# Block-causal attention with a top-2 expert layer: rebuilt with wide q/k rows, exponentials as stationary operand, one scatter of rows, and a dense expert stage in two halves

## Chip, cores and metric

One core of one Trainium2 chip runs the whole program: one launch, inputs in DRAM, output in DRAM. The metric is the device time of one execution in microseconds (us); for the kernel before it is the median of three runs.

## What is computed

The reference in short (B=8, H=8, S=576, D=64; N=4608 tokens, Dm=512, E=8 experts, F=1024):

```python
scores = q @ k.T / sqrt(64)                 # per batch and head
mask   = block_i >= block_j                 # blocks of 64 positions
attn   = softmax(where(mask, scores, -1e9)) @ v
x      = attn as (N, 512)
noisy  = x @ w_gate + log1p(exp(x @ w_noise)) * noise
top2, top2_w = two largest of noisy, softmax over the two
out[n] = sum over both: top2_w * relu(x[n] @ w1[e]) @ w2[e]
```

The inputs are drawn once with a fixed seed. In this draw, with the tokens split by batch into two halves of 2304 (batches 0 to 3, 4 to 7), the largest number of tokens that one expert gets in one half is 624, the smallest 540.

## The kernel before

Everything is scheduled by a tile framework: engines run their own queues, and a tile pool's buffer count sets how far one step may run ahead of the next. The order on each engine's queue is the framework's, made from the code's order and its own estimate of when things are ready.

**Attention** (lines 109 to 205) goes batch by batch. POOL loads q, k and v in 128-row pieces, as 64-element rows per head (L124 to L128, cast to bf16 on the way). PE transposes q and k, two heads at a time (L143, L146), ACT copies the transposes out of PSUM (L149, L151), DVE lays v out with a column of ones (L153, L154). For each head and key tile `jt`, PE makes scores of up to 512 columns with the keys as the stationary operand (L169, contraction over 64 rows, in the lower or the upper row half by the head's parity), ACT takes the exponential (L175) and DVE zeroes the one masked block (L181). L190 then multiplies exponentials (stationary) with v and its ones; DVE divides by the summed column (L197, L198). The rows go to DRAM as `x_bf`.

**Routing** (211 to 347) reads x back tile by tile (L237), transposes it (L240), computes logits (L245), and on six groups of tiles the softplus, the two maxima and the weights. ACT loads function tables as it goes (L252, L253, L272). Positions within each expert come from two matmuls and a scan over all 4608 tokens (L282 to L304). 72 indirect DMAs on POOL write a small record of every token into eight record tables (L329); these are loaded, added and stored as one (L341 to L347).

**Experts** (349 to 435): 8 experts with a capacity of 1280 rows each, in steps of 512, 512 and 256 rows (24 steps, 10240 rows). A step reads its records (L382), gathers its x rows by 128 on POOL (L385), transposes them on PE (L409; ACT copies, L411), computes relu(x w1) with w1 stationary (L417, L420) and the product with w2 (L425), and writes rows to `y_den` (L430, L432). Up to four steps are gathered ahead, and weights come in three buffers (L368, L371).

**Combine** (437 to 453): for each of 36 token tiles POOL gathers two rows per token from `y_den` (L442), DVE scales and adds (L450 to L452), SP writes the output (L453). The gathers stand behind all of `y_den`'s writes.

Of the kernel before, what the change touches and what calls it, by code (L numbers as in the profile page):

```python
# [8 lines left out]
F32 = mybir.dt.float32  # L10
BF16 = mybir.dt.bfloat16
I32 = mybir.dt.int32
U32 = mybir.dt.uint32
AF = mybir.ActivationFunctionType
ALU = mybir.AluOpType


@with_exitstack
def kernel(
# [19 lines left out]

    P = 128  # L40
    NST = (S + P - 1) // P
    s_sizes = [min(P, S - i * P) for i in range(NST)]
    CAP = 1280
    NCT = CAP // P
    BREC = E * CAP + P
    DB = Dm // P
    FB = F // P
    NT = N // P
    NK = 2
    NC = NK * NT  # L50

    x_bf = nc.dram_tensor("x_bf16", (N, Dm), BF16, kind="Internal").ap()
    w1_bf = nc.dram_tensor("w1_bf", (E, Dm, F), BF16, kind="Internal").ap()
    w2_bf = nc.dram_tensor("w2_bf", (E, F, Dm), BF16, kind="Internal").ap()
    bucket_rec = nc.dram_tensor("bucket_rec", (BREC, 4), F32, kind="Internal").ap()
    M = 8
    CHLEN = (NK * (N // P)) // M
    assert (BREC * 4) % P == 0
    BRW = BREC * 4 // P
    rec_m = [nc.dram_tensor(f"rec_m{m}", (BREC, 4), F32, kind="Internal").ap()  # L60
             for m in range(M)]

    consts = ctx.enter_context(tc.tile_pool(name="consts", bufs=1))

    ident_f32 = consts.tile([P, P], F32)
    make_identity(nc, ident_f32)
    ident_bf = consts.tile([P, P], BF16)
    nc.vector.tensor_copy(ident_bf, ident_f32)

    ustrict = consts.tile([P, P], BF16)  # L70
    nc.gpsimd.memset(ustrict, 0.0)
    nc.gpsimd.affine_select(
        out=ustrict, in_=ustrict, compare_op=ALU.is_ge, fill=1.0,
        base=0, pattern=[[-1, P]], channel_multiplier=1,
    )
    ones_mat = consts.tile([P, P], BF16)
    nc.vector.memset(ones_mat, 1.0)

    ecap_i = consts.tile([P, 1, E], I32)
    nc.gpsimd.iota(ecap_i, pattern=[[0, 1], [CAP, E]], base=0, channel_multiplier=0)  # L80
    ecap = consts.tile([P, 1, E], F32)
    nc.vector.tensor_copy(ecap, ecap_i)

    negbig = consts.tile([P, 1], F32)
    nc.vector.memset(negbig, -1.0e9)

    wgn = consts.tile([P, DB, 2 * E], BF16)
    nc.gpsimd.dma_start(out=wgn[:, :, 0:E],
                        in_=moe_w_gate.rearrange("(b p) e -> p b e", p=P))
    nc.gpsimd.dma_start(out=wgn[:, :, E:2 * E],  # L90
                        in_=moe_w_noise.rearrange("(b p) e -> p b e", p=P))

    y_den = nc.dram_tensor("y_den", (E * CAP, Dm), BF16, kind="Internal").ap()

    keep = ctx.enter_context(tc.tile_pool(name="keep", bufs=1))
    boffi_k = keep.tile([P, NC], I32)
    wA_k = keep.tile([P, NK, NT], F32)

    with tc.tile_pool(name="zero", bufs=1) as zpool:
        brz = zpool.tile([P, BRW], F32)  # L100
        nc.vector.memset(brz, 0.0)
        for m in range(M):
            nc.scalar.dma_start(
                out=rec_m[m].rearrange("a b -> (a b)").rearrange("(p w) -> p w", p=P),
                in_=brz)

    x_attn_view = x_bf.rearrange("(b s) (h d) -> b h s d", b=B, h=H)

    with tc.tile_pool(name="qkv", bufs=2) as qkv_pool, \
         tc.tile_pool(name="head", bufs=2) as head_pool, \  # L110
         tc.tile_pool(name="awork", bufs=2) as work_pool, \
         tc.tile_pool(name="xacc", bufs=2) as xacc_pool, \
         tc.tile_pool(name="a_tr_ps", bufs=2, space=bass.MemoryType.PSUM) as tr_psum, \
         tc.tile_pool(name="a_sc_ps", bufs=2, space=bass.MemoryType.PSUM) as sc_psum, \
         tc.tile_pool(name="a_av_ps", bufs=4, space=bass.MemoryType.PSUM) as av_psum:

        for b in range(B):
            q_sb = qkv_pool.tile([P, NST, H, D], BF16, tag="q_sb")
            k_sb = qkv_pool.tile([P, NST, H, D], BF16, tag="k_sb")
            v_sb = qkv_pool.tile([P, NST, H, D], BF16, tag="v_sb")  # L120
            for st in range(NST):
                sl = s_sizes[st]
                ss = st * P
                nc.gpsimd.dma_start(out=q_sb[:sl, st],  # L124
                                  in_=q[b, :, ss:ss + sl, :].rearrange("h s d -> s h d"))
                nc.gpsimd.dma_start(out=k_sb[:sl, st],
                                  in_=k[b, :, ss:ss + sl, :].rearrange("h s d -> s h d"))
                nc.gpsimd.dma_start(out=v_sb[:sl, st],  # L128
                                    in_=v[b, :, ss:ss + sl, :].rearrange("h s d -> s h d"))

            xacc = xacc_pool.tile([P, NST, Dm], BF16, tag="xacc")

            HG = H // 2
            SP = NST * P
            qTa = head_pool.tile([P, HG, SP], BF16, tag="qTa")
            kTa = head_pool.tile([P, HG, SP], BF16, tag="kTa")
            vext5 = head_pool.tile([P, NST, H, D + 1], BF16, tag="vext5")
# [346 lines left out]
```

## Time and profile before

| | us |
|---|---|
| median of three runs (lowest, highest) | 978.03 (977.12, 979.61) |
| span of the profiled execution, first to last instruction | 976.8 |
| PE busy / ACT busy / POOL busy / DVE busy | 629.8 / 412.1 / 343.2 / 243.4 |

The profile is one execution; its page gives no time of its own beside the span, which lies 1.2 us below the median. A busy share is the time in which an engine had an instruction in work. The forty-slice lines show it by stage (a slice is 24.4 us), the chain of waits follows the last instruction back to what it waited for, and the groups by line give the mean duration of one instruction; an idle time has behind it what ended it. PE matmuls overlap in the pipeline, so that a mean duration is longer than the distance from one start to the next.

### The profile page before, as it was taken

What the parts mean: (1) busy time and instruction counts of PE and PEld (TensorE: products, weight loads), DVE (VectorE), ACT (ScalarE), POOL (GpSimd) and SP (SyncE); (2) the same over time, 40 slices, a digit from 0 to 9 for tenths busy, and PEclk for the clock granted to TensorE, in tenths of its full rate; (3) what the DMA queues carried; (4) which work ended last, traced back from release to release, by engine and by line L of the source; (5) the groups of instructions that cost most, each with busy time, mean ns of one, the idle gap of its engine ahead of it and who ended that gap; (6) DMA issues with size and microseconds to landing.
All of it is one profiled execution on the core that took longest, in us unless ns stands there. A gap on an engine that the chain in (4) does not pass through costs nothing.

```text
span 976.8 us, 11092 instructions
## 1 busy us (share of the span) xinstructions
PE 629.8 (64%) x3684; PEld 316.5 (32%) x3684; DVE 243.4 (25%) x1207; ACT 412.1 (42%) x904; POOL 343.2 (35%) x373
## 2 busy tenths in 40 slices
PE   2999999999997550000006899889889888940000
PEld 1544544444443330000002444444444444420000
DVE  1555555555553125000100000000000000015665
ACT  2665565665554781000003555555555555520000
POOL 7945414500000002777434123231312300027775
PEclk9999999999999999999997999999999999985555
DMA  9999849910002320000497372644627210015665
GB/s 132 141 99 79 71 49 88 76 31 25 1 25 55 96 76 1 2 2 2 69 211 138 82 147 73 141 99 108 138 72 146 70 44 33 22 65 178 192 199 172
DMA packets 181578, 84.27 MB, mean 86 GB/s; under 512 B 138128, under 2 KB 167952, under 8 KB 181520
## 3 DMA queue, kind: packets, MB, share of 16 engines
q0 software_dynamic: 135712, 51.04, 40.7%
q1 hardware_dynamic: 33616, 25.13, 8.7%
q10 hardware_dynamic: 12192, 7.38, 2.6%
q8 instruction: 29, 0.48, 0.2%
q14 instruction: 29, 0.24, 0.1%
HBM read 88.18 MB, written 26.28 MB: 117 GB/s over the span
## 4 chain that ended last, share of the span: by engine, by line
PE 56%; issue 13%; ACT 10%; DMA 8%; POOL 8%; DVE 2%; another core or an unknown queue 1%; ACTq 0%; SPq 0%; POOLq 0%; DVEq 0%
PE yp L425 14%; PE hp L417 12%; PE ps L169 12%; PE av L190 11%; POOL rec_m L329 4%; ACT xgT L411 4%; POOL yg L442 3%; DMA yg<-y_den,boffi_k 2%; DMA xt<-x_bf 2%; PE tp L409 2%; DMA xg<-x_bf,gidx 2%; PE tpq L143 2%; ACT esc L175 2%; PE tpk L146 2%; ACT hsb L420 1%
## 5 line engine op out<-in xcount | busy, mean ns | idle before, releaser
L175 ACT ACTIVATE esc<-ps 128x512 bf16<-128x512 f32 (+5 forms) x384 | 140.3, 392 | 112.9 <-PE ps L169 86.4
L417 PE MATMUL hp<-xgT,w1sb 128*128 128x512 bf16 (+1 forms) x768 | 165.2, 350 | 21.0 <-ACT hsb L420 9.6
L385 POOL DMA_INDIRECT xg<-x_bf,gidx x80 | 76.8, 960 | 200.6 <-PE tp L409 102.3
L169 PE MATMUL ps<-qTa,kTa 64*128 64x512 bf16 (+5 forms) x384 | 141.6, 403 | 7.5 <-ACT esc L175 6.3
L190 PE MATMUL av<-vext,esc 128*128 128x65 bf16 (+2 forms) x960 | 143.7, 246 | 0.5 <-DVE xacc L198 0.4
L425 PE MATMUL yp<-w2sb,hsb 128*128 128x512 bf16 x640 | 143.5, 379 | 0.0
L409 PE MATMUL tp<-ident_bf,xg 128*128 128x128 bf16 x320 | 34.7, 222 | 159.5 <-DMA xg<-x_bf,gidx 140.1
L411 ACT ACTIVATE xgT<-tp 128x512 bf16<-128x512 bf16 (+1 forms) x96 | 50.6, 527 | 170.7 <-PE tp L409 161.2
L329 POOL DMA_INDIRECT rec_m<-recA,boffi_k x72 | 70.3, 976 | 144.7 <-DVE boffi_k L323 123.1
L420 ACT ACTIVATE hsb<-hp 128x512 bf16<-128x512 f32 (+1 forms) x192 | 98.6, 526 | 47.8 <-PE hp L417 36.0
L190 PEld LDWEIGHTS <-esc 128*128 128x128 bf16 (+2 forms) x960 | 83.1, 123 | 101.1 <-DVE xacc L198 26.8
L442 POOL DMA_INDIRECT yg<-y_den,boffi_k x72 | 77.0, 1070 | 105.8 <-issue 102.8
L417 PEld LDWEIGHTS <-w1sb 128*128 128x128 bf16 x768 | 72.6, 99 | 81.2 <-issue 36.8
L409 PEld LDWEIGHTS <-xg 128*128 128x128 bf16 x320 | 26.2, 98 | 185.8 <-DMA xg<-x_bf,gidx 140.7
L450 DVE TENSOR_SCALAR acc<-yg,wA_k 128x512 f32<-128x512 bf16 x36 | 18.7, 518 | 271.7 <-DMA yg<-y_den,boffi_k 270.5
L425 PEld LDWEIGHTS <-hsb 128*128 128x128 bf16 x640 | 62.5, 98 | 73.5 <-issue 0.9
L430 ACT ACTIVATE ysb<-yp 128x512 bf16<-128x512 f32 x80 | 47.8, 598 | 88.9 <-PE yp L425 88.9
L198 DVE TENSOR_SCALAR xacc<-av,denom 128x64 bf16<-128x64 f32 (+1 forms) x320 | 82.3, 276 | 5.0
L197 DVE RECIPROCAL denom<-av 128x1 f32<-128x1 f32 (+1 forms) x320 | 52.4, 165 | 105.7 <-PE av L190 102.4
L128 POOL DMA_DIRECT2D v_sb<-in_v_dram x40 | 36.0, 901 | 60.7 <-DVE xacc L198 60.7
L169 PEld LDWEIGHTS <-kTa 64*128 64x128 bf16 (+1 forms) x384 | 35.5, 108 | 34.2 <-issue 14.1
L124 POOL DMA_DIRECT2D q_sb<-in_q_dram x40 | 35.9, 897 | 24.2 <-PE ps L169 12.8
(81 smaller groups left out, 392.2 us busy)
## 6 DMA issues: line engine op xcount, KB each, us to landing
out_dram<-acc SPq DMA_DIRECT2D x36, 256.0 KB
w1sb<-in_moe_w_dram POOLq DMA_DIRECT2D x8, 1024.0 KB
w2sb<-in_moe_w_dram POOLq DMA_DIRECT2D x8, 1024.0 KB
y_den<-ysb SPq DMA_DIRECT2D x40, 128.0 KB
y_den<-ysb ACTq DMA_DIRECT2D x40, 128.0 KB
xt<-x_bf SPq DMA_DIRECT2D x36, 128.0 KB
q_sb<-in_q_dram POOLq DMA_DIRECT2D x32, 128.0 KB
k_sb<-in_k_dram POOLq DMA_DIRECT2D x32, 128.0 KB
```

The lines of the kernel that those rows point to most:

```text
L169: nc.tensor.matmul(out=ps[:jl, :cn], lhsT=kTa[po:po + D, g, jt * P:jt * P + jl], rhs=qTa[po:po + D, g, i0 + off:i0 + off + cn], start=True ...
L175: nc.scalar.activation(out=esc[:jl, jt, off:off + cn], in_=ps[:jl, :cn], func=AF.Exp, scale=1.0 / (D ** 0.5),)
L190: nc.tensor.matmul(out=av[:il, :], lhsT=esc[:jl, jt, loc:loc + il], rhs=vext5[:jl, jt, h, :], start=(jt == 0), stop=(jt == ib),)
L198: nc.vector.tensor_scalar_mul(xacc[:il, ib, h * D:(h + 1) * D], av[:il, 0:D], denom[:il])
L329: nc.gpsimd.indirect_dma_start(out=rec_m[m], out_offset=bass.IndirectOffsetOnAxis(ap=boffi[:, c:c + 1], axis=0), in_=recA_f[:, c, :], in_o ...
L385: nc.gpsimd.indirect_dma_start(out=xg[:, ci, :], out_offset=None, in_=x_bf, in_offset=bass.IndirectOffsetOnAxis(ap=gidx[:, ci:ci + 1], axi ...
L409: nc.tensor.transpose(tp[:, ci * P:(ci + 1) * P], xg[:, ci, db * P:(db + 1) * P], ident_bf)
L411: nc.scalar.activation(out=xgT[:, db, 0:QW], in_=tp[:, 0:QW], func=AF.Copy)
L417: nc.tensor.matmul(out=hp[:, 0:QW], lhsT=w1sb[:, db, fb * P:(fb + 1) * P], rhs=xgT[:, db, 0:QW], start=(db == 0), stop=(db == DB - 1))
L420: nc.scalar.activation(out=hsb[:, fb, 0:QW], in_=hp[:, 0:QW], func=AF.Relu)
L425: nc.tensor.matmul(out=yp, lhsT=hsb[:, fb, ci * P:(ci + 1) * P], rhs=w2sb[:, fb, :], start=(fb == 0), stop=(fb == FB - 1))
L442: nc.gpsimd.indirect_dma_start(out=yg[:, kk, :], out_offset=None, in_=y_den, in_offset=bass.IndirectOffsetOnAxis(ap=boffi_k[:, c:c + 1], a ...
```

## The change

The program is written anew. Two batches make a group `g` (four groups), two groups make a half.

- q and k are loaded as contiguous rows of 512 elements, which hold eight successive positions of one head. PE transposes 64x128 pieces so that batch 2g lands in row half 0 and batch 2g+1 in row half 64; DVE copies 1024 columns at a time and undoes the interleaving of positions by a strided write (new line 172). v is loaded straight into its tile with the ones.
- Scores of the two batches alternate between the two row halves of PE (new line 233) into one PSUM tile of 2 x 512 columns, on which ACT takes one exponential of 1024 elements a partition (237). Key tiles of 320 and 192 columns share a tile. AV accumulates four heads in one PSUM tile (261, and 275 for the last 64 positions), DVE divides four heads at once.
- The rows of a group stay in SBUF (`xr`). Router transposes (288), logits (292), and positions (one matmul pair and one scan a group, with a running base per half) follow at once. `exp` and `ln` come from one preloaded table; the second weight is the reciprocal of 1 plus an exponential.
- Each token's row is scattered by two indirect DMAs a tile (357; 72 in all) directly into expert buckets of 640 rows, one DRAM array `xd` a half. SP writes zeros over both arrays at the start (2 x 5.2 MB), so that unused rows hold zeros. Rows beyond 640 would go to an overflow area.
- Experts run dense: for each half and expert one plain load of 640 rows (380), 20 transposes (392), four DVE copies of 640 columns (393), 64 matmuls of 320 columns (399), 40 of 512 (407), DVE copies (410), SP writes. All weights stay in SBUF: experts 0 and 1 in their own space, loaded during attention, 2 to 7 in space that attention held.
- The combine of half 0 is issued after its eighth expert, that of half 1 at the end (36 gathers each, line 419; two DVE operations a tile, 424 and 425).
- At the end the largest count is loaded into a register, and a branch computes overflow rows if it is above 640.

The core of the diff (the whole of the old body goes):

```diff
+    for lo, hi in ((0, 1), (4, 6), (1, 4), (6, 9)):
+        nc.gpsimd.dma_start(out=qr[:, lo:hi, :], in_=qv[:, t0 + lo:t0 + hi, :])
+        nc.gpsimd.dma_start(out=kr[:, lo:hi, :], in_=kv[:, t0 + lo:t0 + hi, :])
...
+    nc.tensor.transpose(tp[64 * hf:64 * hf + 64, r * n:(r + 1) * n],
+                        raw[p0:p0 + n, src_t, r * 64:(r + 1) * 64],
+                        ident[p0:p0 + n, p0:p0 + n])
...
+    for u in range(3):
+        sc = sc_ps.tile([P, 2, 512], F32, tag="sc")
+        for jt, a, z, off in pieces[u]:
+            for hf in range(2):
+                c0 = col0(hf, h)
+                sl = slice(64 * hf, 64 * hf + 64)
+                nc.tensor.matmul(out=sc[:, hf, off:off + z - a],
+                                 lhsT=kT[sl, c0 + jt * P:c0 + jt * P + P],
+                                 rhs=qT[sl, c0 + a:c0 + z], start=True, stop=True)
+        nc.scalar.activation(out=esc[:, hh, :, u * 512:(u + 1) * 512], in_=sc,
+                             func=AF.Exp, scale=scale)
...
+    ins = nc.gpsimd.indirect_dma_start(
+        out=xd[half], out_offset=bass.IndirectOffsetOnAxis(
+            ap=slots[:, t0 + idx, i:i + 1], axis=0),
+        in_=xr[:, idx, :], in_offset=None, bounds_check=XR - 1, oob_is_err=False)
...
+    seq = [(half, e) for half in range(NH) for e in range(E)]
+    xgs = {0: load_x(*seq[0]), 1: load_x(*seq[1])}
+    for e in range(2, E):
+        load_w(wL, e)
+    for i, (half, e) in enumerate(seq):
+        if i + 2 < len(seq):
+            xgs[i + 2] = load_x(*seq[i + 2])
+        expert(half, e, xgs.pop(i))
+        if i == E - 1:
+            combine(0)
+    combine(1)
+    over = nc.values_load(flag_i[0:1, 0:1], min_val=0, max_val=1)
+    with tc.If(over > 0):
...
```

Two places of the order. On POOL's queue, from the end of attention on, before (`rec_m` are the record tables, `xg` an expert step's x rows, `yg` the combine's rows):

```order
L221 IOTA recA 128x72
L329 DMA rec_m<-recA,boffi_k 10368x4 x72
L368 DMA w1sb<-in_moe_w_dram 128x4x1024
L371 DMA w2sb<-in_moe_w_dram 128x8x512
L368 DMA w1sb<-in_moe_w_dram 128x4x1024
L371 DMA w2sb<-in_moe_w_dram 128x8x512
L385 DMA xg<-x_bf,gidx 128x512 x20
```

and now, from the scatters of groups 1 and 2 on:

```order
L357 DMA xd<-xr,slots 9728x512 x36
L115 DMA w_2_3721<-in_moe_w_dram 128x4x1024
L117 DMA w_2_3723<-in_moe_w_dram 128x8x512
L115 DMA w_3_3725<-in_moe_w_dram 128x4x1024
L117 DMA w_3_3727<-in_moe_w_dram 128x8x512
L357 DMA xd<-xr,slots 9728x512 x18
L115 DMA w_4_3729<-in_moe_w_dram 128x4x1024
...
L117 DMA w_7_3743<-in_moe_w_dram 128x8x512
L419 DMA yg<-yd,gslots 128x512 x72
```

The 72 indirect writes of a stage of their own became 72 scatters that stand group by group between the loads, the 80 gathers of x rows are gone, and all 72 combine gathers follow the last weight load. On DVE's queue, at the first combine, before (behind the last expert step's index conversion):

```order
L383 CAST gidx<-brt 128x4 x2
L383 CAST gidx<-brt 128x2
L450 TENSOR_SCALAR acc<-yg,wA_k 128x512
L451 TENSOR_SCALAR tmp<-yg,wA_k 128x512
L452 TENSOR_TENSOR acc<-acc,tmp 128x512
```

and now, between the x copies of the first expert of half 1 and those of the second:

```order
L393 COPY xgT<-tp 128x640 x4
L424 TENSOR_SCALAR acc<-yg,wts 128x512
L425 SCALAR_TENSOR_TENSOR acc<-yg,wts,acc 128x512
...
L424 TENSOR_SCALAR acc<-yg,wts 128x512
L410 CAST ysb<-yp 128x512
...
L410 CAST ysb<-yp 128x512
L425 SCALAR_TENSOR_TENSOR acc<-yg,wts,acc 128x512
L393 COPY xgT<-tp 128x640 x4
L410 CAST ysb<-yp 128x512 x5
```

All 36 operations of the first combine (18 tiles) stand there in one run, with the five `ysb` casts of one expert among them, the first behind the eighth tile, and the x copies of the next expert (`xgT`) behind all of them.

## Rows read from the trace of the kernel before

**Rows 1.** Page, the span in 40 slices: PE and its granted clock, in tenths.

```profile
PE   2999999999997550000006899889889888940000
PEclk9999999999999999999997999999999999985555
```

**Rows 2.** Windows by stage: length, then busy us (instructions) of PE, PEld, DVE, ACT, POOL; PEclk, DMA share, GB/s.

```profile
25.00:150.00 125.00, 122.25 (x738) 61.42 (x736) 65.86 (x415) 76.83 (x206) 63.92 (x78) 1.00 1.21 89
310.00:382.00 72.00, 30.79 (x292) 19.41 (x292) 22.21 (x86) 44.99 (x71) 0.00 (x0) 1.00 0.27 73
382.00:480.00 98.00, 0.00 (x0) 0.00 (x0) 1.02 (x3) 0.00 (x0) 70.26 (x72) 1.00 0.10 15
600.00:700.00 100.00, 89.78 (x514) 45.80 (x512) 0.34 (x2) 55.71 (x111) 28.62 (x31) 1.00 0.49 109
868.00:977.00 109.00, 0.40 (x2) 0.00 (x0) 59.00 (x108) 0.60 (x1) 77.02 (x72) 0.51 0.55 176
...
500.00:540.00 40.00, 20.07 (x78) 8.35 (x79) 2.56 (x14) 8.80 (x16) 15.51 (x17) 0.83 0.94 171
```

**Rows 3.** Chain of waits in order of time: start us, us, what.

```profile
9.02 0.89 POOL q_sb L124
...
491.64 19.01 DMA xg<-x_bf,gidx
...
551.37 6.92 PE yp L425 x32
561.46 1.03 PE hp L417 x8
...
604.33 1.03 PE hp L417 x8
...
869.07 1.70 DMA y_den<-ysb
...
969.05 3.18 DMA yg<-y_den,boffi_k
```

**Rows 4.** Groups by line and shape: busy us, mean ns of one, idle before and releasers.

```profile
L190 PE MATMUL av<-vext,esc 128*128 128x65 bf16 x640 | 101.1, 241 | 0.0
L169 PE MATMUL ps<-qTa,kTa 64*128 64x512 bf16 x64 | 38.7, 604 | 0.0
L175 ACT ACTIVATE esc<-ps 128x512 bf16<-128x512 f32 x64 | 38.3, 598 | 50.6 <-PE ps L169 31.1 <-issue 5.5 <-ACT esc L175 5.2
L175 ACT ACTIVATE esc<-ps 128x64 bf16<-128x64 f32 x64 | 14.2, 222 | 14.7 <-PE ps L169 13.2
L409 PE MATMUL tp<-ident_bf,xg 128*128 128x128 bf16 x320 | 34.7, 222 | 159.5 <-DMA xg<-x_bf,gidx 140.1 <-ACT xgT L411 19.4
L143 PE MATMUL tpq<-ident_bf,q_sb 128*128 128x128 bf16 x128 | 23.1, 304 | 16.3 <-DMA q_sb<-in_q_dram 16.3
L198 DVE TENSOR_SCALAR xacc<-av,denom 128x64 bf16<-128x64 f32 x256 | 65.6, 277 | 3.5
L294 DVE COPY scanA<-tot_ps 128x576 f32<-128x576 f32 x1 | 0.8, 750 | 0.0
L256 DVE TENSOR_TENSOR noisy<-noisy,lg 128x48 f32<-128x48 f32 x6 | 1.2, 204 | 0.6
```

**Rows 5.** Timeline of PE within attention: start us, us, engine, line, what.

```profile
109.96 0.34 PE L190 MATMUL av<-vext,esc 128*128 128x65 bf16 x3
110.24 0.26 PE L169 MATMUL ps<-qTa,kTa 64*64 64x64 bf16 x1
...
112.29 0.23 PE L169 MATMUL ps<-qTa,kTa 64*128 64x64 bf16 x1
112.29 0.23 PE L143 MATMUL tpq<-ident_bf,q_sb 64*128 64x64 bf16 x1
```

**Rows 6.** Timeline of POOL, first and last of the 72 combine gathers.

```profile
871.79 1.02 POOL L442 DMA_INDIRECT yg<-y_den,boffi_k  x1 [84.21 <-issue]
...
969.05 1.39 POOL L442 DMA_INDIRECT yg<-y_den,boffi_k  x1 [0.31 <-issue]
```

More of the change, by code (lines that the diff above doesn't have):

```diff
@@ L87 @@
[L87 to L97, printed above, removed]
@@ new lines, with token_rows @@
+    NG = B // 2
+    TG = 9
+    NT = NG * TG
+    NH = 2
+    TH = NT // NH
+    CAP = 640
+    CT = CAP // P
+    NW = CAP // 2
+    OVB = E * CAP
+    XR = OVB + 2 * TH * P
+    BIG = float(1 << 20)
+    SET = 4
+    EO = (0, 576, 1024, 1344)
+    ESC = 1536
+    scale = 1.0 / (D ** 0.5)
+    xd = [nc.dram_tensor(f"xd{i}", (XR, Dm), BF16, kind="Internal").ap() for i in range(NH)]
+    yd = [nc.dram_tensor(f"yd{i}", (OVB, Dm), BF16, kind="Internal").ap() for i in range(NH)]
+    def token_rows(g, idx):
+        if idx < 8:
+            b = 2 * g + idx // 4
+            return [(0, P, b * S + (idx % 4) * P)]
+        return [(64 * hf, 64, (2 * g + hf) * S + 512) for hf in range(2)]
@@ new lines, with setup_consts @@
+    ecap_i = consts.tile([P, E, 1], I32)
+    rmask = consts.tile([P, E, TG], F32)
+    ovrow_i = consts.tile([P, 2, TH], I32)
+    ovrow = consts.tile([P, 2, TH], F32)
+    base = [consts.tile([P, E, 1], F32, name=f"base{i}") for i in range(NH)]
+    nz_all = keep.tile([P, NT, E], F32)
+    slots = keep.tile([P, NT, 2], I32)
+    gslots = keep.tile([P, NT, 2], I32)
+    wts = keep.tile([P, 2, NT], F32)
+    oh_all = keep.tile([P, NG, 2, E, TG], BF16)
+    zero = keep.tile([P, 2048], BF16)
+    def setup_consts():
+        make_identity(nc, ident_f)
+        nc.vector.tensor_copy(ident, ident_f)
+        nc.gpsimd.memset(prem, 0.0)
+        nc.gpsimd.affine_select(out=prem, in_=prem, compare_op=ALU.is_gt, fill=-1.0,
+                                base=0, pattern=[[1, P]], channel_multiplier=-1)
+        nc.vector.memset(ones_mat, 1.0)
+        nc.gpsimd.iota(ecap_i, pattern=[[CAP, E], [0, 1]], base=0, channel_multiplier=0)
+        nc.vector.tensor_copy(ecap, ecap_i)
+        nc.vector.memset(rmask, 1.0)
+        nc.vector.memset(rmask[:, :, 0:1], 0.0)
+        nc.gpsimd.iota(ovrow_i, pattern=[[TH * P, 2], [P, TH]], base=OVB, channel_multiplier=1)
+        nc.vector.tensor_copy(ovrow, ovrow_i)
+        for i in range(NH):
+            nc.vector.memset(base[i], 0.0)
@@ L437 @@
[L437 to L453 removed]
+            mx = rt.tile([P, 2, TG, 1], F32, tag="mx")
@@ new lines @@
+            nc.vector.reduce_sum(sl2, pk.rearrange("p i e t -> p i t e"), axis=AX.X)
+            tl = (g % 2) * TG
+            nc.vector.tensor_tensor(out=sl2, in0=sl2, in1=ovrow[:, :, tl:tl + TG], op=ALU.min)
+            nc.vector.tensor_scalar(gslots[:, t0:t0 + TG, :].rearrange("p t i -> p i t"), sl2,
+                                    float(OVB - 1), None, op0=ALU.min)
+            nc.vector.tensor_copy(slots[:, t0:t0 + TG, :].rearrange("p t i -> p i t"), sl2)
+            for idx in range(TG):
+                for i in range(2):
+                    ins = nc.gpsimd.indirect_dma_start(
+                        out=xd[half], out_offset=bass.IndirectOffsetOnAxis(
+                            ap=slots[:, t0 + idx, i:i + 1], axis=0),
+                        in_=xr[:, idx, :], in_offset=None,
+                        bounds_check=XR - 1, oob_is_err=False)
+                    key = f"scat{half}"
+                    tc.declare_no_dep(ins.ins, group=key, reason="rows of one half are distinct") if scat[half] else None
+                    tc.add_to_no_dep_group(key, ins.ins)
+                    scat[half].append(ins.ins.name)
```

661 lines of the change are left out of this document (308 added, 353 removed).

## The prediction

> **What bounds the kernel now.** I read the forty slices first. PE is full in slices 2 to 12, half used for three slices, empty for four or five, near nine tenths for fourteen, and empty in the last four [rows 1]. The windows put lengths on this [rows 2]: attention keeps PE at 122 of 125 us; routing uses it for 31 of 72; from 382 to 480 us PE does nothing and POOL issues 72 record writes; the experts hold it at 90%; from 868 on PE is idle again and POOL's 72 gathers take 77 of 109 us. So five stages stand one behind the other, and the chain of waits passes through each: record writes, a 19.01 us x gather behind the first weight loads, PE through the experts, the last `y_den` write, the combine gathers [rows 3]. A gain must come from a shorter PE stage or from a stage moved beside PE. The groups by shape [rows 4] give the prices, the timelines the spacing of matmuls [rows 5] and of gathers [rows 6].
>
> One reading decides how attention is priced. The granted clock reads 1.00 there [rows 2], yet a 128x128 transpose took 304 ns in attention and 222 ns in the experts [rows 4]. A score of 512 columns took 604 ns. I therefore take attention's columns at the 1.2 GHz level and the experts' at 2.4, as these rows have them.
>
> The Trainium skill (TensorE: Matmul & The Clock Gate, Part 1) says that a busy PE is brought to 2.4 GHz; the 122 busy us of 125 at the slow durations do not agree with it, and it returns below as a rival.
>
> **The start.** POOL's first q load starts at 9.02 us [rows 3], behind constants and two small loads. Now q and k come first; eight loads at 0.89 us, then the identity, put the first transpose at about 9.5 us (estimate). The 10.5 MB of zeros cost nothing if they flow beside this: at the 176 GB/s of the combine window [rows 2] they need 60 us of DMA time, and what they hide behind is group 0's PE work. Without that cover I allow 0 to 20 us more.
>
> **Attention, four groups.** Before, two batches took about (310 - 12)/4 = 74 us [rows 2]. PE's work in a group: 24,576 score columns (8 heads x 2 batches x 1,536: 20.5 us at 1.2 GHz, 10.2 if the two row halves run together), 240 AV products, 160 + 36 transposes, 36 logits. AV products of one shape start 0.05 us apart (three in 0.34, one in 0.24) and a change of shape costs about 0.11 more: the score behind those three starts at 110.24, 0.18 after the last of them [rows 4, 5]. That is 240 x 0.054 = 13 us for AV, 15.4 for q/k transposes at 128 columns in 0.107 us, or 8 if their two column halves run together, 6 for the router, and 80 x 0.11 = 9 for changes of shape. PE's sum is 46 us with halves together and 63 with none.
>
> Do halves run together? At 112.29 a 64-row score and a 64-row transpose start in the same hundredth [rows 5], while two AV products on the whole array never start closer than 0.05. I take the halves as concurrent.
>
> The Trainium skill (TensorEngine Tiling, Key Properties) says that different tiles of the array run in parallel and that a change of tiling mode drains the engine; both agree with these two rows.
>
> Walked through in the new order, a group goes in four phases. A: the q/k copies on DVE. By L294 (750 ns for 576 elements from PSUM) and L198 (277 for 64), a copy of 1024 is 1.2 us: eight of these, two of 512 and two small ones are 11.5; 25 router operations of the group before at 0.2 us (L256) stand among them: 16.5 us. B: scores of heads 2 and 3, six exponentials of 1024; by the 598 and 222 ns of 512 and 64 elements one costs 1.03 us: 6.5 with the small one. C: AV of four heads beside scores of two (PE, 11.4), then six exponentials (6.2): 17.6. D: AV of the other four heads and the router's transposes and logits: 14. Sum **54.6 us a group**; four end at 9.5 + 218 = **228 us**. Both bounds (46 and 64 us a group) go into the range.
>
> **What leaves the path here.** Routing's reload, its table loads, the 98 us of record writes, their merge and the gathers [rows 2] have no successor on PE's path: 18 scatters a group take 18 x 1.3 = 23 us of POOL, beside the next group. Weights of experts 0 and 1 load during group 3. The first expert needs half 0 only, scattered two groups earlier; it waits for the SBUF of the last AV products, not for the router of group 3 (6 us, beside it). A 640 KB load then takes about 7 us (before: four weight loads and a gather within 19.01 [rows 3]). PE starts experts at 228 - 6 + 7 = **229 us**. The other six weight pairs need about 9.5 us each by the same row, against 20 us of PE per expert: hidden; if the x loads queue behind them, up to 10 us more.
>
> **Experts, half 0.** Columns and rows stay as they were: 10240 rows. Before, one expert of 1280 rows in three steps took 604.33 - 561.46 = 42.87 us [rows 3]. Its products are 36.8 (32 `yp` in 6.92, so 0.216 for 512 columns, and the rest in proportion), so 2.0 us a step is lost while transposes and copies precede the first `hp`. Now two steps: 36.8 + 2 x 2.0 = 40.9, or **20.45 a step**. DVE makes four copies of 640 columns (0.8 us each by L294) where ACT made four of 512 (0.6), so I keep the 2.0. Eight steps: 163.6. Leaving idleness costs clock: from 500 to 540 it read 0.83, a loss of 6.8 us [rows 2]. 229 + 6.8 + 163.6 = **400 us**.
>
> **Combine of half 0.** Here a new wait appears. DVE's queue holds all 36 combine operations ahead of the x copies of the second expert of half 1, and the first of them waits for a gather that waits for all of half 0's writes. From the last product: 0.6 (cast), 1.70 (write), 36 gathers 1.37 apart ((969.05 - 871.79)/71 [rows 6]) = 49.3, landing 3.18 [rows 3], last operations 1.2: **56 us**, in which PE can do only one expert and stalls 36. At 456 the other seven follow: 143.2, and again 6.8 for the clock: **606 us**.
>
> **End.** Combine of half 1, by the same sum 56, the last output write and the flag about 3: **665 us** of span. The profiled span of before stands 1.2 us below the median of its runs, so I forecast **666 us**: 312 below 978. Stage by stage: attention 310 - 228 = 82; from there to the first expert product 202 less 1 (it started near 512, where the x gather landed); experts 356 less 341, so 15; the tail 108 less 59, so 49; against these the 36 of the stall.
>
> **Rivals.**
> 1. *Halves do not run together* (13%). For: alternation in every row pair is new here, and the only evidence is four instructions at one place. Then the other 10.2 us of scores in each group come on top, little of it covered in C and D: +40, **706 us**.
> 2. *PE runs attention at 2.4 GHz* (20%). For: copies and scores are fewer and larger. Against: PE was 97% busy before and did not. C and D shrink by about 5.6 a group, A and B are bound by DVE and ACT: -22, and one clock loss less, **637 us**.
> 3. *The first combine stalls little* (9%): if gathers or DVE ran through quicker than POOL's 1.37 us each, or the casts let PE go on. At most -36, **630 us**.
> 4. *The start is bound by DMA, or loads at the boundary queue up* (10%): zeros share DMA engines with q, k and v; +20 to +40, **695 us**.
> 5. *The overflow branch runs* (2%), the other side. It decides at 641 rows for one expert in one half; the draw's largest is 624, so rounding in the logits would have to move 17 tokens. Its price: 36 tiles x 8 experts x (32 products of 128 columns at 0.054 + 8 of 512 at 0.216 = 3.5 us) = 1,000 us on top: **1,670 us**, slower than before.
> 6. *Something in the new stages costs over 300 us* (1%), such as the row order making PE wait for every copy: no row speaks for it.
>
> **How the numbers follow.** The forecast holds 45%. Its terms each carry some 10 us (DVE's strided copies, clock losses, gather spacing). The range takes rivals 2 and 3 below and 1 and 4 above: **610 to 725 us**. A difference under 0.3% (3 us) cannot be told from no change here; every case but 5 and 6 lies far beyond it: faster 0.96, same 0.01, slower 0.03.
>
> **What would show it.** Right: first AV near 30 us, expert stage from about 229, steps of 20 to 21 us, a hole of some 36 us in PE behind the second-half's first expert with DVE waiting for `yg`, a tail of 56 us. Wrong: scores in the two halves starting one full score apart (rival 1); transposes at 222 ns in attention (rival 2); a chain through output writes or zero writes (rival 4); PE products behind the flag's load (rival 5).

## The result and the profile after

The changed kernel takes **728.26 us** (median of 4 runs, 722.25 to 730.25) beside 978.82 us for the kernel before: a ratio of 0.7428, 95% interval [0.7397, 0.746]. The prediction, 666 us in a range of 610 to 725, had the direction right and the size too good by 62 us; the result lies 3 us above its range.

The page of the changed kernel: span, then of the forty slices (18.2 us each) PE, POOL, the granted clock and what the DMA engines moved.

```profile
span 726.5 us, 10418 instructions
...
PE   2087788361786284039999999964179999996000
...
POOL 5126625777004413370000000077600000001773
PEclk9988866555566566559999999995589999999555
...
GB/s 207 343 231 169 181 195 177 142 124 101 1 2 60 73 15 260 210 133 221 226 125 73 71 55 59 72 176 200 150 105 73 73 73 37 37 37 46 177 192 146
```

Against [rows 1] the long empty stretch in the middle is gone, but PE has new weak places: slice 2, slices 8 to 18, and slices 27 to 30. In slices 10 and 14 PE is busy for one and two tenths, while the DMA engines move 101 and 73 GB/s; in slice 3 they move 231 and PE is at eight tenths. So full DMA engines are not what PE waits for there.

The chain of waits names the places (start us, us, what).

```profile
6.21 29.41 DMA kr<-in_k_dram
35.91 19.55 DMA vt<-in_v_dram
...
120.72 14.83 another core or an unknown queue
...
166.89 13.31 another core or an unknown queue
...
234.13 13.25 another core or an unknown queue
...
346.65 8.63 PE yp L407 x40
...
375.51 8.62 PE hp L399 x63
384.13 8.65 PE yp L407 x40
...
515.88 9.01 another core or an unknown queue
531.74 9.83 PE hp L399 x64
...
657.30 8.65 PE yp L407 x40
```

At the start the chain is DMA for 49 us. In attention it runs through a releaser that the trace doesn't show. From 347 to 470 us and from 532 to 666 us it is PE almost alone, with two products an expert, as in [rows 3] but without the gaps; between the two stretches and behind the second stand the combines. In the totals of the waits (engine, line and its releaser: us in all, times, longest), "remote" is the releaser not shown.

```profile
ACT esc L237 <- remote: 48.8, 5, 14.6
...
DVE rden L278 <- remote: 41.7, 6, 13.3
ACT hsb L402 <- DMA xd<-xr,slots: 39.5, 1, 39.5
...
DVE ysb L410 <- remote: 9.0, 1, 9.0
```

In the timeline, the 18 scatters of group 0 are on POOL from 122.65 to 145.6 us. PE makes the scores of group 2 at 127.19 us, but ACT's exponential of them starts only at 135.57 us. In a later run of the same kernel that has no such waits (e16 below), the same scores stand at 127.20 us and ACT starts at 127.84, so here ACT is 7.7 us late; the other 6.5 us of its idle time are there too. From 139 us on, one transpose of PE starts every 0.70 us or twice that, where 16 took 1.06 us at 126.19.

```profile
127.19 1.03 PE L233 MATMUL sc<-qT,kT 64*128 64x512 bf16 x4
...
135.57 1.02 ACT L237 ACTIVATE esc<-sc 128x1024 bf16<-128x1024 f32 x1 [14.61 <-remote]
...
139.05 0.27 PE L166 MATMUL tp<-ident,kr 128*64 128x128 bf16 x1 [1.10 <-issue]
139.75 0.27 PE L166 MATMUL tp<-ident,kr 128*64 128x128 bf16 x1 [0.43 <-issue]
```

In the timeline of ACT at 319 us, the first relu of expert 0 has waited 39.55 us for the scatters of group 3.

```profile
318.97 1.30 ACT L402 ACTIVATE hsb<-hp 128x640 bf16<-128x640 f32 x2 [39.55 <-DMA xd<-xr,slots]
```

I call the first effect **the hold-up**: while POOL issues row-wise (indirect) DMAs back to back, what PE does gets through late. In the four sessions on the chip that gave the result and runs e1 to e10, every run with unpaced scatters shows it (the kernel before took 979 to 987 us there); in the four sessions of e11 to e18 (973 to 974 us) no run does, though the scatters of e11 and e12, one of these sessions, were all paced.

### The profile page after: what moved, and what is told of

The parts are those of the page before. It is cut to its first block, busy times and chain, and to the rows that moved or that the text cites. A ratio compares the mean times of both kernels' runs of the same rounds, so it can differ in the third digit from the quotient of the medians.

```text
span 726.5 us, 10418 instructions
## 1 busy us (share of the span) xinstructions
PE 472.7 (65%) x4264; PEld 292.6 (40%) x4264; DVE 253.3 (35%) x591; ACT 187.3 (26%) x245; POOL 218.7 (30%) x244
## 2 busy tenths in 40 slices
DMA packets 102902, 91.62 MB, mean 126 GB/s; under 512 B 49088, under 2 KB 86976, under 8 KB 102848
## 4 chain that ended last, share of the span: by engine, by line
PE 50%; issue 12%; DMA 9%; another core or an unknown queue 9%; POOL 7%; DVE 7%; ACT 6%; POOLq 0%; DVEq 0%; ACTq 0%; SPq 0%
PE hp L399 18%; PE yp L407 18%; ACT esc L237 6%; POOL yg L419 4%; DMA kr<-in_k_dram 4%; PE av L261 4%; DMA vt<-in_v_dram 3%; PE sc L233 2%; PE av L275 2%; POOL xd L357 2%; PE tp L392 2%; PE tp L166 2%; DVE ysb L410 1%; PE tp L288 1%
## 5 line engine op out<-in xcount | busy, mean ns | idle before, releaser
L399 PE MATMUL hp<-xgT,w 128*128 128x320 bf16 x1024 | 149.9, 305 | 33.6 <-ACT hsb L402 33.6
L419 POOL DMA_INDIRECT yg<-yd,gslots x72 | 75.6, 1050 | 317.6 <-PE hp L399 149.4
L402 ACT ACTIVATE hsb<-hp 128x640 bf16<-128x640 f32 x128 | 89.9, 703 | 288.7 <-PE hp L399 246.6
L407 PE MATMUL yp<-w,hsb 128*128 128x512 bf16 x640 | 146.4, 388 | 17.8 <-DVE ysb L410 14.8
L399 PEld LDWEIGHTS <-w 128*128 128x128 bf16 x1024 | 101.5, 100 | 74.8 <-issue 34.0
L410 DVE CAST ysb<-yp 128x512 bf16<-128x512 f32 x80 | 55.3, 691 | 212.3 <-PE yp L407 203.3
L237 ACT ACTIVATE esc<-sc 128x1024 bf16<-128x1024 f32 x96 | 91.5, 1036 | 127.8 <-PE sc L233 72.2
L357 POOL DMA_INDIRECT xd<-xr,slots x72 | 71.0, 986 | 92.8 <-DVE slots L352 46.9
L233 PE MATMUL sc<-qT,kT 64*128 64x512 bf16 (+4 forms) x320 | 52.8, 376 | 29.4 <-ACT esc L237 27.4
L261 PE MATMUL av<-vt,esc 128*128 128x65 bf16 x640 | 42.6, 234 | 38.5 <-DVE xr L279 29.7
L261 PEld LDWEIGHTS <-esc 128*128 128x128 bf16 x640 | 34.4, 123 | 52.9 <-DVE xr L279 35.1
L424 DVE TENSOR_SCALAR acc<-yg,wts 128x512 f32<-128x512 bf16 x36 | 19.0, 529 | 35.8 <-DMA yg<-yd,gslots 31.1
```

What stands on the lines that cost most here:

```text
L233: nc.tensor.matmul(out=sc[:, hf, off:off + z - a], lhsT=kT[sl, c0 + jt * P:c0 + jt * P + P], rhs=qT[sl, c0 + a:c0 + z], start=True, stop=True)
L237: nc.scalar.activation(out=esc[:, hh, :, u * 512:(u + 1) * 512], in_=sc, func=AF.Exp, scale=scale)
L261: nc.tensor.matmul(out=av[:, hh, :], lhsT=esc[:, hh, hf, c:c + P], rhs=vb[:, 4 * hf + jt, h, :], start=(jt == 0), stop=(jt == ib))
L357: ins = nc.gpsimd.indirect_dma_start(out=xd[half], out_offset=bass.IndirectOffsetOnAxis(ap=slots[:, t0 + idx, i:i + 1], axis=0), in_=xr[:, ...
L399: nc.tensor.matmul(out=hp[:, n, 0:NW], lhsT=w1sb[:, db, fb * P:(fb + 1) * P], rhs=xgT[:, db, n * NW:(n + 1) * NW], start=(db == 0), stop=( ...
L402: nc.scalar.activation(out=hsb[:, fb, :].rearrange("p (n w) -> p n w", n=2), in_=hp[:, :, 0:NW], func=AF.Relu)
```

## The experiments

Each ratio is to the kernel before in the same session; 0.01 is about 9.8 us. Those to compare with are 0.7428 up to e10 and, from e11 on, 0.6885 (e16).

### The hold-up

**e2**: plain DMAs to consecutive rows in place of the scatters.

```diff
-  nc.gpsimd.indirect_dma_start(out=xd[half], out_offset=...slots..., in_=xr[:, idx, :])
+  nc.gpsimd.dma_start(out=xd[half][r0:r0 + P, :], in_=xr[:, idx, :])
```

> Edit: each of the 72 indirect scatters becomes a plain DMA of the same 128 rows x 1 KB from the same queue (POOL) to consecutive rows of xd, so rows are not sorted by expert (the routing of rows is left out; all later work keeps its size). Theory B (PE's completions are seen late only while POOL issues indirect DMAs): the waits without known releaser in groups 2 and 3 (together 56 us on the chain) go, and expert 0 starts some 8 us earlier since plain issues take 0.87 us instead of 1.29: about 660 us. Rival C (any DMA traffic or any burst of POOL's DMAs does this): they stay, 715 to 728 us. Rival D (those waits come from buffers, not from POOL): they stay too, at the same places.

Measured: 627.41 us, 0.6357 [0.6321, 0.6393]. No unshown waits in attention; the groups' last AV products are 45 to 46 us apart. In the first combine, where indirect gathers stayed, waits of 1.91 and 8.82 us on an unshown releaser remain. Against the changed kernel this is about 105 us less, the 39.5 us wait of the first relu included. Not all of it is the price of the row-wise issue: the edit also takes the index tile away, so that a group's writes no longer wait for its router, and the last 18 now stand ahead of the weight loads on POOL (200 to 211 us). The parts were not separated.

**e6**: the scatters stay, their rows are dropped.

```diff
-  bounds_check=XR - 1, oob_is_err=False
+  bounds_check=0, oob_is_err=False
```

> The bound of the 72 scatters is set to row 0, so that the queue drops every row but those for slot 0: POOL issues the same 72 instructions with the same index tiles, and nearly no packet goes out. The rows of the experts stay zero, and so does the result: the routing of rows is left out. Theory B3: PE's completions are held up by POOL's working through the row lists. Then the waits of ACT and DVE on an unshown releaser stay at 70 to 95 us and the ratio stays at 0.72 to 0.74. Theory B4: they are held up by the packets (128 rows of 1 KB per DMA). Then these waits vanish as with plain DMAs (0.6357), attention ends near 207 us, and the ratio is 0.63 to 0.66.

Measured: 729.32 us, 0.7398 [0.7363, 0.7433], no gain. The expectation was wrong on one point: the number of packets stayed at 102902, only their bytes fell, from 91.62 to 82.22 MB. So neither the 9.4 MB of rows nor the places where they land are the cause. The number of packets is not either, since e2 has 102902 of them too. What e6 keeps and e2 takes away is the issue by index, row by row. The waits of the run:

```profile
DVE rden L278 <- remote: 39.1, 6, 13.4
DVE ysb L410 <- remote: 13.7, 2, 8.9
DVE kT L172 <- remote: 10.7, 1, 10.7
```

**e5** and **e10**: a POOL operation behind each scatter, of 1024 elements or of one.

```diff
+  nc.gpsimd.tensor_copy(zero[:, 0:1024], slots[:, t0 + idx, i:i + 1].to_broadcast([P, 1024]))
```

> Behind each of the 72 scatters stands one POOL copy of 1024 elements into the zeros' tile, which nothing reads any more; the result is unchanged. Scatters now come some 2.5 to 3 us apart, not 1.29. Theory B1: PE's completions come late only while row-wise DMAs follow each other without a gap (POOL's path of 18 in a row). Then the waits of ACT and DVE on a releaser the trace doesn't show (ACT esc 48.8 us, DVE rden 41.7 us) fall below 20 us together, attention's last V products end near 215 us, not 276; but 72 scatters then take some 200 us of POOL from 122 us on, so the last lands near 330 us and the first relu, which still waits for it, comes 10 to 25 us later than 319: ratio 0.74 to 0.77. Theory B2: each row-wise DMA costs its share wherever it stands. Then those waits stay near 90 us in all, spread over more of the stretch, and the ratio is 0.76 to 0.80.

> As the paced run, but the POOL copy behind each scatter has one element a partition instead of 1024, so the scatters come some 1.4 to 1.5 us apart and not 2.19. Theory B1a: what lets PE's completions through is any POOL compute operation between two row-wise DMAs. Then the waits on an unshown releaser in the attention stage are under 10 us in all (paced: 0), groups 2 and 3 get their loads earlier than in the paced run, and the ratio is 0.67 to 0.715. Theory B1b: it is the lower rate, or the time POOL is off the row lists. Then these waits stay above 60 us and the ratio is 0.735 to 0.75.

Measured: e5 714.37 us, 0.7247 [0.7206, 0.7287]; e10 724.99 us, 0.738 [0.7339, 0.742]. In e5 no unshown wait is left in attention. Its POOL, in the timeline, issues a scatter every 2.2 us:

```profile
126.99 1.03 POOL L357 DMA_INDIRECT xd<-xr,slots  x1 [0.18 <-issue]
128.02 1.04 POOL L362 CAST zero<-slots 128x1024 bf16<-128x1024 int32 x1
129.23 0.98 POOL L357 DMA_INDIRECT xd<-xr,slots  x1 [0.17 <-issue]
```

In e10, at 1.34 us, ACT still waits 46.9 us and DVE's `rden` 38.5. So another POOL operation between two scatters is not enough; what helps is the lower rate, or the longer time between them. e5 gains only 18 us, since POOL is then the slow engine: k and v loads of group 2 stand behind 18 paced scatters, its first AV set ends at 173.8 us, and the wait of the first relu grows to 50.0 us.

**e16**: the changed kernel again, unaltered, in a later session.

> The changed kernel once more, not a line of it altered, on another of the chips, beside the next run. With the pools in another order all waits on an unshown releaser were gone from the attention stage although the scatters came 1.29 us apart as ever (0.6775), and that run and the two before it were on chips on which the kernel before took 973 and 974 us, where it took 979 to 987 us on those with such waits. Theory L (the order of the pools did it): this run shows 80 to 110 us of these waits again, 0.735 to 0.75, whatever the next one does. Theory H (it differs from chip to chip or from load to load): this run has or lacks them as the next one does; without them 0.68 to 0.71.

Measured: **669.80 us** (4 runs, 667.91 to 671.36), 0.6885 [0.6859, 0.6912], and not one wait on an unshown releaser. Its page (span, PE by slices of 16.7 us) and its waits:

```profile
span 668.3 us, 10418 instructions
...
PE   2077878848888501999999999631899999993000
```

```profile
ACT hsb L402 <- DMA xd<-xr,slots: 39.4, 1, 39.4
DVE xr L279 <- DMA xd<-xr,slots: 7.0, 1, 7.0
```

PE is busy through attention; the wait of the first relu is as long as before. The hold-up thus needs a condition outside the kernel. I saw it hold within a session and change between sessions, with the same chip listed for one of each kind; what it is stays open. The traces differ in one more way: those of e11 to e18 give a time from issue to landing for the scatters (2.4 us in e16), those of all other runs give none. Every timed run was recorded, so whether the recording takes part in the hold-up is not shown. So e13, which suggested that the order of the pools removes the hold-up, only fell into a session without it.

### The start

**e3**: the zeros are made on POOL and written behind the first loads of V.

```diff
-  nc.vector.memset(zero, 0.0); (zero writes); load_v(0)
+  load_v(0); nc.gpsimd.memset(zero, 0.0); (zero writes)
```

> Edit: the zero tile is set on POOL behind the issue of group 0's v loads, so that the 10.5 MB of zero writes start after q, k and v are under way. Theory E (the start is bound by DMA, rival 4 of the prediction): k's second load, which landed at 35.6 us, comes within 15, v within 30, and the first AV set ends near 50 us instead of 56; 15 to 22 us less, about 708 us. Rival F (q, k and v themselves are slow, or the zeros only move the wait to the loads of group 1): 5 us less or nothing, about 724 us.

Measured: 710.64 us, 0.72 [0.7179, 0.7221]. In its chain the first k rows take 11.49 us instead of 29.41, and the first AV set ends at 39.9 instead of 57.8 us. The zeros shared the DMA engines with q, k and v, and cost 18 us at the start and 22 us of the run.

```profile
6.20 11.49 DMA kr<-in_k_dram
```

### The first expert's wait

The activations `hsb` overlap the tile `xr` of the last group by 448 bytes a partition, and the last 18 scatters read `xr`. **e1** moves `hsb`, **e13** also the outputs, **e18** puts the later experts' weights (which POOL loads behind the scatters anyway) over `xr`.

```diff
-  pools: wL, xgp, xgtp, hp, yp, fin
+  e1:    wL, xgp, xgtp, yp, fin, hp
+  e13:   wL, hp, xgtp, fin, yp, xgp
+  e18:   xgp, xgtp, hp, yp, wL, fin
```

> Edit: only the order of the SBUF pools of the expert stage, so that the first hidden tile (hsb) shares no byte with the rows (xr) of group 3; in the changed kernel the two share 448 bytes a partition. Theory A (that overlap alone holds back expert 0, whose first relu waited 39.6 us until group 3's scatters had landed): expert products run on from about 281 us instead of 319, so 36 us less, about 692 us. Rival B (while POOL issues indirect DMAs one behind the other, what PE has finished is seen late by ACT and DVE): the wait for the scatters goes, but ACT's relus still come late between 284 and 317 us; gain at most 10 us, about 718 us or more, with ACT idle put down to no known releaser.

> Only the order of the experts' pools in SBUF is another: the tiles of the combines, which are first written long after the attention stage, now lie where the last group's rows lie, and none of the first experts' activations (hsb) or outputs (ysb) does. The earlier order only moved the wait: there DVE's first output copy waited 24.1 us for the same scatters. Theory C: the overlap is a term of its own. Then no engine waits for the last group's rows, the first relu is at about 287 us as in the earlier run, the first output copy at 297 to 300 instead of 320, and the ratio is 0.705 to 0.72. Theory B: while 18 scatters are issued nothing of PE's gets through, whatever waits. Then the first experts stand still until the scatters end at 317, with the wait under another name (an unshown releaser), and the ratio is 0.725 to 0.735, as before.

Measured: e1 719.66 us, 0.7292 [0.7271, 0.7313]; e13 660.26 us, 0.6775 [0.6761, 0.6789], against 0.6885 for e16. Each order only handed the wait on: in e1 DVE's first output copy waits 24.1 us for the scatters, in e13 DVE's first `xgT` copy:

```profile
249.42 0.89 DVE L393 COPY xgT<-tp 128x640 bf16<-128x640 bf16 x2 [25.46 <-DMA xd<-xr,slots]
```

> As the run of three edits, but the later experts' weights, which POOL loads behind the last scatters anyway, lie where the attention stage's rows lie, and the experts' rows and activations lie lower; nothing of the first two experts waits for the last group's scatters any more (in the run before it DVE's first xgT copy waited 24.7 us, after the same wait had stood at the activations and at the output rows). Theory C: the overlap is a term of its own. Then the first products of expert 0 come at 220 to 228 us instead of 252, of which some 8 us may be lost again to the weights of expert 2, now behind the scatters: 595 to 605 us, a ratio of 0.61 to 0.622. If something else holds the first experts at 250 us: 0.63 to 0.64. With the waits on an unshown releaser back, add 50 to 70 us.

Measured: **593.33 us** (592.62 to 593.82), 0.6094 [0.6075, 0.6112], 27 us below the run before it (e17, 0.6367), which has the other edits. PE goes from the last router products into the first expert without a hole:

```profile
214.47 0.27 PE L292 MATMUL lg<-wgn,xT 128*128 128x16 bf16 x4
215.17 0.27 PE L292 MATMUL lg<-wgn,xT 128*128 128x16 bf16 x4 [0.43 <-DVE xT L290]
215.30 1.97 PE L392 MATMUL tp<-ident,xg 128*128 128x128 bf16 x15
217.06 0.74 PE L400 MATMUL hp<-xgT,w 128*128 128x320 bf16 x2
```

So the overlap is a term of its own. Another wait of the same kind remains: in group 2, DVE waits 19.7 us to write `xr`, which the scatters of group 0 still read. Expert 2 then waits 2.62 us for its weights, as feared, though less.

### The first combine

**e4** gives its arithmetic to POOL; **e7** cuts it into six pieces of three tiles, whose gathers follow the first write of an expert of half 1; **e9** lets a piece's gathers follow that expert's `xgT` copies, and its DVE operations those of the next.

```diff
-  if i == E - 1: combine(0)
+  if 0 < j <= 6:  combine(0, 3 * j - 3, 3 * j, held, cut)     # e9, j = i - E; cut: the last xgT copy
+  if 0 <= j < 6:  held = gather(0, 3 * j, 3 * j + 3, cut)
```

> Edit: the arithmetic of the first combine moves from DVE to POOL (three operations a tile in place of two, 5 ysb buffers in place of 6 for the room). Theory G (as predicted: the 36 combine operations ahead of the next x copies on DVE's queue stall PE): PE's gap behind the first expert of half 1 goes, 60.5 us from its start to the next become some 21, about 688 us. Rival B (PE's completions are seen late while POOL issues the 36 gathers): the gap shrinks by less than 25 us, about 705 us or more.

Measured: 751.35 us, 0.7613 [0.7591, 0.7635], slower, for a reason neither theory had. POOL needs 4.4 us a tile (1573, 1572 and 1269 ns) where DVE needs 1.28 (529 and 748 ns); SP's output writes wait for POOL (112.4 us in all), the experts' own writes stand behind them in SP's order, and DVE waits for their buffers:

```profile
DVE ysb L411 <- DMA yd<-ysb: 89.3, 10, 36.8
```

> The first combine is cut into six pieces of three row tiles; piece j waits for the first output write of expert j of half 1, so its 6 gathers and 6 DVE operations (3 x 1.24 us) lie beside that expert. Theory F: the 60.5 us between the last products of half 0 and the first transposes of half 1 are DVE standing in its order behind gathers. Then about 60.5 - 20 = 40 us go, the pieces cost 0 to 2 us each, and the ratio is 0.70 to 0.715. Theory G: gathers hold up the experts wherever they stand, also six at a time. Then each piece adds 4 to 7 us to its expert step (19.3 becomes 24 to 26) and the ratio stays at 0.725 to 0.745.

Measured: 736.11 us, 0.7467 [0.7434, 0.75], no gain, and steps of 27 us. It looks like theory G, but the timeline of DVE says otherwise: in each piece DVE waits for `yg`, with `ysb` and `xgT` copies that PE needs standing behind. From 480 to 650 us PE's transposes wait 35.1 us in all for `xgT`.

```profile
524.02 0.49 DVE L429 TENSOR_SCALAR acc<-yg,wts 128x512 f32<-128x512 bf16 x1 [1.00 <-DMA yg<-yd,gslots]
524.42 0.48 DVE L393 COPY xgT<-tp 128x640 bf16<-128x640 bf16 x1
525.61 0.75 DVE L430 SCALAR_TENSOR_TENSOR acc<-yg,wts,acc 128x512 f32<-128x512 bf16 x1 [0.71 <-DMA yg<-yd,gslots]
```

> The first combine in six pieces again, but a piece's 6 gathers wait for the last transposed-row copy (xgT) of expert j of half 1 and its 6 DVE operations for that copy of expert j+1, one step of 19.3 us later. Theory F (DVE standing in its order behind gathers that are not there yet): now none is waited for, the steps of half 1 stay at 19.3 to 20.5 us, the 60.5 us fall to about 20, and the ratio is 0.695 to 0.715. Theory G (gathers hold up the experts wherever they stand): the steps are 24 us and more, as with the pieces right behind an expert's first write (27 us), and the ratio is 0.73 to 0.75.

Measured: 688.05 us, 0.7004 [0.6983, 0.7024]: 41 us gained with the same number of gathers, and with the DVE operations one step later. In its chain the steps of half 1 are 19.29 us from one to the next:

```profile
471.65 8.62 PE hp L400 x63
480.27 8.65 PE yp L408 x40
488.94 0.69 DVE ysb L411
490.94 8.62 PE hp L400 x63
```

### Together

> The three edits together: the activations' tile of the experts away from the last group's rows, the zeros written behind the first loads of V, and the first combine in six pieces. If the three gains are independent (13, 22.5 and some 40 us), 733 - 75 = about 658 us, a ratio of 0.66 to 0.675. If the early start only moves attention's end into the same wait for the scatters, the gain of the zeros is lost for the most part: 0.685 to 0.70.

Measured (e1, e3, e7 together): 706.21 us, 0.7164 [0.7124, 0.7203]; 26 us less, where e1 and e3 alone gave 13 and 22 and e7 took 4.

> Four edits together: the experts' activations away from the last group's rows, the zeros behind the first loads of V, one POOL copy of 1024 elements behind each scatter, and the first combine in six pieces one step later. If the causes found are the causes and do not cover each other: no waits on an unshown releaser in the attention stage; attention's last V products at about 225 us (238 in the paced run, 13 to 18 us earlier by the start; POOL, with 18 scatters of 2.19 us and 18 loads a group, then sets a group at about 55 us instead of 45); experts right behind at 230 to 240, 16 steps of 19.3 us with little at 1.2 GHz to about 550, tail 60: 600 to 625 us, a ratio of 0.61 to 0.635. If the scatters stay in the way of the first expert although its tile is apart (the rows of half 0 land late, or POOL is fuller than reckoned): 640 to 670 us, 0.65 to 0.68.

> As the run of four edits, but the POOL copy has 512 elements, so the scatters come some 1.7 to 1.8 us apart, between the freeze at 1.29 and 1.34 us and none at 2.19. If the hold-up sets in only at the full rate, it stays away, POOL needs 46 us a group instead of 55, and the time is 15 to 30 us below the run of four edits: a ratio of 0.59 to 0.61. If it grows with the rate, waits on an unshown releaser of 10 to 40 us come back in the attention stage and the two runs are within 10 us of each other, or this one is slower.

Measured (e1, e3, e9 and the POOL copies): e11 641.68 us, 0.6587 [0.6559, 0.6616]; e12, copies of 512 elements, 627.39 us, 0.6449 [0.6419, 0.6479]. The sessions had no hold-up, so they don't tell the rate from which it sets in. DVE waits 36.6 and 31.4 us there for the scatters that still read the `xr` which group 2 (and 3) is to fill. What pacing costs without the hold-up shows by e14 and e17 below, which differ in the copies alone: 0.657 against 0.6367, about 20 us.

> The run of four edits with the copies of 512 elements (0.6449), with this order of the pools in place of the earlier one. Theory C: the 32.0 us for which DVE's first output copy waited for the last group's rows go, as far as nothing else takes their place; some 28 us less, a ratio of 0.61 to 0.625. If the late scatters hold something else (the next wait in line), 0.63 to 0.645.

> The run before it, and the weights of experts 0 and 1 are loaded behind the first group's scatters instead of ahead of them on POOL. In the run of four edits these scatters began at 114.5 us though their rows were there before 106, and DVE waited 31.4 us at 152 us for the buffer of the rows that they read. If the weight loads' place in POOL's queue is what makes the scatters late, they begin 5 to 12 us earlier, that wait shrinks by as much, and the ratio falls by 0.005 to 0.012 below the run before it. If the loads of V and of q and k set POOL's start, it stays within 0.003 of it.

Measured: e14 (e12 with the order of e13) 640.13 us, 0.657 [0.6559, 0.6581]: slower than e12, since `xgT` (35.5 us) is a worse place for the wait than `ysb` (32.0): in e12, PE has made the first expert's `hp` products when the wait ends at 279 us, in e14 it makes its first at 270.8. e15 634.6 us, 0.6521 [0.6504, 0.6537]: without weight loads ahead of them on POOL the first scatters start at 103 instead of 114 us.

> The new order of the pools, the zeros behind the first loads of V, the first combine in six pieces one step later; no POOL copies between the scatters. Where no waits on an unshown releaser come up: 660 us of the run with the order alone, less some 22 us at the start and 40 us at the first combine, about 600 us: 0.61 to 0.63. Where they do: 0.65 to 0.68.

Measured (e13, e3, e9; no copies): 620.22 us, 0.6367 [0.6339, 0.6395]. The 40 us of the combine came; the gain of the start was lost in group 2. Group 1's last AV set ends 17 us earlier than in e13 (101.1 for 117.8 us), but then DVE waits for the scatters of group 0 that still read `xr`, and group 2's first AV set ends no earlier (154.9 for 154.4 us). The wait, in e13 5.9 us:

```profile
DVE xr L279 <- DMA xd<-xr,slots: 22.7, 1, 22.7
```

With the wait of the first experts gone, e18 is the fastest version.

## Why the prediction was wrong, and where it was right

The table has the prediction's own steps, cut at the starts and ends of instructions in the traces, in us; "again" is e16, the same kernel without the hold-up.

| step | predicted | measured | again |
|---|---|---|---|
| start and group 0, to its last AV | 58 | 71.8 | 71.8 |
| three more groups, to the last AV | 164 | 197.8 | 143.2 |
| last AV to first relu | 9 | 49.3 | 49.2 |
| half 0, to its last output cast | 168 | 151.0 | 149.5 |
| first combine, to the next expert's transposes | 57 | 60.5 | 56.7 |
| the other seven experts | 150 | 135.5 | 136.6 |
| tail | 59 | 60.5 | 61.3 |

**The step that failed** is "18 scatters a group take 18 x 1.3 = 23 us of POOL, beside the next group". The size is right (1.29 us each), "beside" is not: where the hold-up is, three groups take 54.6 us more (197.8 less 143.2), some of it at a lower clock (granted 0.52 from 119 to 201 us, 0.70 from 117 to 169 us in e16). That POOL's issue of the scatters is what does it is shown by e2, e5 and e6, within sessions that have the hold-up; why those sessions have it stays open. None of the rivals had it. A trace of it was there before the change. The chain of the kernel before has, within the experts and at the end of a long run of x gathers, these rows:

```profile
520.47 1.49 another core or an unknown queue
522.58 5.73 another core or an unknown queue
```

The 72 record writes of [rows 2], the nearest rows for the scatters, could not show it: PE was idle there.

**The second step** is "it waits for the SBUF of the last AV products, not for the router of group 3". The wait is for SBUF, but for the rows that the last scatters read: 40 us. The prediction noted that POOL is busy with scatters and that weights load; that the loads of experts 2 and 3 (issued from 270 to 273 us) stand ahead of the last 18 scatters on POOL, and these scatters ahead of the first expert, it did not. The weights of experts 0 and 1 did not load during group 3 either, but were issued from 81.8 us on, in group 1.

**Mis-sized terms.** The zeros "cost nothing", with up to 20 us allowed: they cost 18 to 22 (e3), though in e17 the time that their later place gave was lost again in group 2. A group was put at 54.6 us; in e16 it takes 45 (53 where DVE waited 7 us for `xr`). The durations were right (DVE's copy of 1024 1.23 us for 1.2, ACT's 1.036 for 1.03); the sum laid phases A to C end to end, which partly overlap, and PE ran part of a group at the higher clock (0.75 granted from 75 to 119 us, where a score of 512 columns takes 476 ns; from 140 to 160 us it takes 593 at a granted 0.50), so rival 2 came true in part. The same durations settle the reading on which attention was priced: 604 ns in [rows 4] is the 1.2 GHz level, as the prediction took it. The 1.00 that [rows 2] gives beside it is no measurement: the first record of the clock in the trace of the kernel before stands at 515.8 us, and a stretch without a record reads 1.00, also from 382 to 480 us, where PE did nothing. The rule of the Trainium skill (TensorE: Matmul & The Clock Gate, Part 1), a busy PE at 2.4 GHz, fits only in part: in e16 the granted clock from 117 to 215 us is 0.70. The expert step, put at 20.45 us with 2.0 lost ahead of the first `hp`, takes 19.29.

**Right** were the first combine as a wait of DVE, its mechanism (e9) and its size, the tail, and the overflow branch not taken. Rival 1 did not come: the four scores at 127.19 us take 1.03 us together, where one alone takes 0.59 at the same granted clock. Rival 4 came true as to the start only. The 669.80 us of e16 stand near 666 by errors that cancel: +14 and +40 against -21, -19 and -13.

## What to carry to other kernels

An engine's work "beside" another is free only if a row shows that the other went on at its pace meanwhile; a stage in which the other idled proves nothing. Before a moved step is put beside the next stage, follow its buffers into that stage: a scatter late in a queue holds the SBUF that the next pools are laid over, and moving one tile hands the wait to the next. In an in-order queue, operations that wait for gathers are to be placed one step behind the gathers, not right after them.

## What the runs showed of the hardware

- Indirect DMAs issued 1.29 to 1.34 us apart by POOL held up the other engines and made three groups of attention 54.6 us longer; at 2.2 us apart (e5) they held up nothing in attention, nor did plain DMAs from the same engine (e2). Dropping the rows' 9.4 MB (e6) changed nothing. The same program took 728 us with the hold-up and 670 without it, in sessions whose difference is not known.
- A scatter of 128 rows of 1 KB took POOL 0.98 us, and landed 2.42 us after the start of its issue (the chain of e18). The Trainium skill (Perfetto Trace Analysis, DMA Instruction — SWDGE (GPSIMD)) says that the profile's end of such an instruction is the end of descriptor writing, not of the transfer; these two numbers agree.
- POOL takes 1.57 us for a multiplication by a scalar of 512 elements a partition (e4, L427), where DVE takes 0.53 (the result, L424).
- PE was busy for 122.25 of 125 us in the attention of the kernel before, at durations of the 1.2 GHz level (a score of 512 columns 604 ns; 593 ns at a granted 0.50 in the result).
